# Stationary operands of 64 rows or columns widened to 128 in a pooled attention and ReGLU kernel

## Chip, cores, metric

One core of one Trainium2 chip. The metric is the device time of one execution in microseconds (us), the lower the better. All executions used here are of the fast state; the granted TensorE clock was 0.997 to 1.0 in every profile.

## The reference, cut to what matters

```python
# q, k, v: (8 batches, 8 heads, 576 rows, 64), float32
k_p = k.reshape(B, H, 72, 8, D).mean(axis=3)      # pooled: 72 keys, 72 values per head
v_p = v.reshape(B, H, 72, 8, D).mean(axis=3)
attn = softmax(q @ k_p.T / 8)                     # 576 x 72 per head
x = (attn @ v_p), heads side by side              # 4608 x 512
out = (relu(x @ w_gate) * (x @ w_val)) @ w_out    # 512 -> 1536 -> 512
```

576 rows are four full pieces of 128 and one left piece of 64. The left piece is what this study is about.

## The kernel before: the parts that matter

`P` is 128, `SP` 72, `REST` 64, `n_pc` 5; piece 4 is the left piece. A matmul's `lhsT` is its stationary operand: its partitions are the rows, its free elements the columns.

```python
def weights(b, h, t):                       # exponentials: 72 rows, n columns
    n = piece_size(t)                       # 128, or 64 for the left piece
    if b == 0:
        return pieces[t][:SP, h, :n]
    return exp_tiles[b, h][:SP, t * P:t * P + n]

def pool_v_array(b, half):                  # batches 0 and 1: values pooled on TensorE
    ...
        terms = [(sel_main, main[:, hs, t, :]) for t in range(KG)]
        terms.append((sel_rest[:P // 2], rest[:, hs, :]))      # 64 rows
    ...

def values(b, t, halves=(0, 1)):
    n = piece_size(t)
    ...
            nc.tensor.matmul(
                out=ps[:n, c0:c0 + D + 1], lhsT=weights(b, h, t),
                rhs=stats[b % 2][:SP, g, s0:s0 + D + 1], start=True, stop=True)
    ...                                     # VectorE: reciprocal of the sums, product -> x

def back(b, t, eng):                        # x transposed into x_T
    x, n = x_tiles.pop((b, t)), piece_size(t)
    ...
    if eng is nc.sync:                      # batches 2 to 7 (but three full pieces of 2): by DMA
        eng.dma_start_transpose(out=dst, in_=x)
        return
    for g in range(NG):
        nc.tensor.transpose(out=ps[:, g, :n], in_=x[:, g, :], identity=ident16[:n, :n])
    ...

# the order in the first batch's products, where batch 1 is prepared
run([z[3], z[4], z[5], lambda: pool_k_wide(1, 2, nc.vector), a[6], qt[0], a[7], qt[1], qt[2], kt, ...])
```

`a` and `z` are products of the gate and value matrices for the halves of the first 512 tokens, `qt` transposes of batch 1's queries, `kt` the pooling of its keys on TensorE.

The softmax here doesn't subtract the row's maximum and nothing guards it: scores larger than these inputs give would overflow.

Of the kernel before, what the change touches and what calls it, by code (L numbers as in the profile page):

```python
# [11 lines left out]
F32 = mybir.dt.float32  # L12
F16 = mybir.dt.float16
AF = mybir.ActivationFunctionType
ALU = mybir.AluOpType
# [3 lines left out]
def kernel(  # L19
# [10 lines left out]
    nc = tc.nc  # L30

    B, H, S, D = q.shape
    POOL = 8
    SP = S // POOL
    DM = H * D
    DFF = moe_w_gate.shape[1]
    NTOK = B * S
    P = 128
    NG = H // 2
# [35 lines left out]
    row_pool = ctx.enter_context(tc.tile_pool(name="rowp", bufs=4))  # L75
# [16 lines left out]
    ident16 = const_pool.tile([P, P], F16, name="ident16")  # L92

    sel_main = const_pool.tile([P, SP], F16, name="sel_main")
    sel_rest = const_pool.tile([P, SP], F16, name="sel_rest")
# [20 lines left out]
    REST = 2 * RI * QP  # L116
# [5 lines left out]
    def full_at(b):  # L122
        return b * S + (REST if b % 2 else 0)

    def rest_at(b):
        return b * S + (0 if b % 2 else FULL)
# [27 lines left out]
    KG = POOL // 2  # L154
# [4 lines left out]
    def load_k_wide(b):  # L159

        tl = kin_pool.tile([P, KJ, POOL, D], F16, name="k_in").rearrange("p j t d -> p (j t d)")
        flat = k[b].rearrange("h (p t) d -> (h p) (t d)", p=QP)
        thirds = [slice(i * K_THIRD, (i + 1) * K_THIRD) for i in range(3)]
        k_tiles[b] = [tl[:, cols] for cols in thirds]
        if b:
            nc.gpsimd.dma_start(out=tl[:, :QT * D], in_=flat)
            return
        for i, cols in enumerate(thirds):
            eng = nc.gpsimd
            if i < 2:  # L170
                eng = nc.sync
                k_tiles[b][i] = sum_pool.tile([P, n_hf, TCH // 2], F16, name=f"sum{i}").rearrange(
                    "p f t -> p (f t)")[:, :2 * K_THIRD].bitcast(F32)
            eng.dma_start(out=k_tiles[b][i], in_=flat[:, cols])

    def load_v_wide(b):
        tl = wo_sums.rearrange("p x f d -> p (x f d)")
        n = H * KG * D
        main = tl[:, :n].rearrange("p (h t d) -> p h t d", h=H, d=D)
        rest = tl[:P // 2, n:n + H * D].rearrange("p (h d) -> p h d", h=H)  # L180
        v_tiles[b] = (main, rest)
        nc.gpsimd.dma_start(
            out=main.rearrange("p h t d -> p h (t d)"),
            in_=v[b].rearrange("h (x t) d -> x h (t d)", t=KG)[:P])
        nc.gpsimd.dma_start(
            out=rest, in_=v[b].rearrange("h r d -> r h d")[P * KG:])

    def load_q(b, i0=0, n=NI):
        if b not in q16_tiles:
# [131 lines left out]
    def queries(b, h, i0=0, n=NI):  # L321
        return qT_tiles[b][:, i0:i0 + n, h * QP:(h + 1) * QP]

    exp_tiles = {}
# [28 lines left out]
    def weights(b, h, t):  # L353

        n = piece_size(t)
        if b == 0:
            return pieces[t][:SP, h, :n]
        return exp_tiles[b, h][:SP, t * P:t * P + n]

    def pool_v_array(b, half):  # L360

        ps = ps_mm.tile([P, HH, D], F32, name="mm_ps", tag="mm_ps")
        hs = slice(half * HH, (half + 1) * HH)
        if b:
            main, rest = v_tiles[b]
            terms = [(sel_main, main[:, hs, t, :]) for t in range(KG)]
            terms.append((sel_rest[:P // 2], rest[:, hs, :]))
        else:
            terms = [(sel_first[:SP], v_tiles[b][:SP, hs, t, :]) for t in range(POOL)]
        for i, (sel, rows) in enumerate(terms):  # L370
            nc.tensor.matmul(  # L371
                out=ps[:SP], lhsT=sel, rhs=rows, start=(i == 0), stop=(i == len(terms) - 1))
        g0 = half * NG // 2
        st = stats[b % 2][:SP, g0:g0 + NG // 2, :]
        st = st.rearrange("p g (x d) -> p g x d", d=D)[:, :, 0::3, :]
        src = ps[:SP].rearrange("p (g x) d -> p g x d", x=2)
        if b or half:
            nc.scalar.copy(st, src)
        else:
            nc.vector.tensor_copy(out=st, in_=src)  # L380

    pieces, x_tiles, value_tiles = {}, {}, {}

    def piece_size(t):
        return P if t < 2 * NF else REST

    def piece_scores(t):
        n, j = divmod(t, 2)
        cols = [(j, n * IQ, IQ)] if n < NF else [(0, NF * IQ, RI), (1, NF * IQ, RI)]
        e = row_pool.tile([P, DM], F32, name="row").bitcast(F16).rearrange("p (h t) -> p h t", h=H)  # L390
        for half in range(2):
            ps = ps_mm.tile([P, HH, P], F32, name="mm_ps", tag="mm_ps")
            for r in range(HH):
                h, c0 = half * HH + r, 0
                for j, i0, cnt in cols:
                    nc.tensor.matmul(
                        out=ps[:SP, r, c0:c0 + cnt * QP], lhsT=kpTs[0][j][:, h, :],
                        rhs=queries(0, h, i0, cnt), start=True, stop=True,
                    )
                    c0 += cnt * QP  # L400
            nc.scalar.activation(
                out=e[:SP, half * HH:(half + 1) * HH, :c0], in_=ps[:SP, :, :c0], func=AF.Exp,
                scale=EXP_SCALE)
        pieces[t] = e

    def values(b, t, halves=(0, 1)):


        n = piece_size(t)
        W = 2 * D + 4  # L410
        if halves[0] == 0:
            value_tiles[b, t] = (piece_pool.tile([P, NG, 2, D], F16, name="px"),
                                 piece_pool.tile([P, 2, NG // 2, 2], F32, name="prd"))
        x, rd = value_tiles[b, t]
        for half in halves:
            ps = ps_at.tile([P, 512], F32, name="at_ps", tag="at_ps")
            for h in range(half * HH, (half + 1) * HH):
                g, hh = divmod(h, 2)
                c0 = g % (NG // 2) * W + hh * (D + 1)
                s0 = 3 * D - 1 if hh else 0  # L420
                nc.tensor.matmul(  # L421
                    out=ps[:n, c0:c0 + D + 1], lhsT=weights(b, h, t),
                    rhs=stats[b % 2][:SP, g, s0:s0 + D + 1], start=True, stop=True,
                )
            pv = ps[:n, :NG // 2 * W].rearrange("p (g c) -> p g c", c=W)
            nc.vector.reciprocal(out=rd[:n, half], in_=pv[:, :, D:D + 2])
            nc.vector.tensor_tensor(  # L427
                out=x[:n, half * NG // 2:(half + 1) * NG // 2, :, :],
                in0=pv.rearrange("p g (x c) -> p g x c", x=2)[:, :, :, :D],
                in1=rd[:n, half].unsqueeze(3).to_broadcast([n, NG // 2, 2, D]), op=ALU.mult)  # L430
        x_tiles[b, t] = x[:n].rearrange("p g x d -> p g (x d)")

    def back(b, t, eng):


        x, n = x_tiles.pop((b, t)), piece_size(t)
        x0 = rest_at(b) if t == n_pc - 1 else full_at(b) + t * P
        dst = x_T[:, :, x0 % RING:x0 % RING + n]
        if eng is nc.sync:
            eng.dma_start_transpose(out=dst, in_=x)  # L440
            return
        ps = ps_mm.tile([P, NG, P], F16, name="mm_ps", tag="mm_ps")
        for g in range(NG):
            nc.tensor.transpose(out=ps[:, g, :n], in_=x[:, g, :], identity=ident16[:n, :n])  # L444
        if eng is nc.scalar:
            eng.copy(dst, ps[:, :, :n])
        else:
            eng.tensor_copy(out=dst, in_=ps[:, :, :n])

    h_tiles = {}  # L450

# [72 lines left out]
    wo_sums = const_pool.tile([P, 3, n_hf, HD], F16, name="wo_sums")  # L524
# [592 lines left out]
    def clear_other(half):  # L1117

        upper = any(half is pair[1] for pair in kpTs)
        nc.vector.memset(half[:D] if upper else half[D:], 0.0)  # L1120

    def ones(i):

        two = stats[i].rearrange("s g d -> s (g d)").bitcast(F32).rearrange(
            "s (g d) -> s g d", g=NG)
        nc.vector.memset(two[:SP, :, D // 2:3 * D // 2], TWO_ONES)
# [23 lines left out]
    with tc.manual_schedule():  # L1150
        nc.scalar.preload_act_table_set("natural_log_exp_and_others")
        nc.vector.memset(warm_sb, 0.0)
        for half in kpTs[0]:
            clear_other(half)
        ones(0)
        load_k_wide(0)
        make_identity(nc, ident16)
        load_q(0, 0, IQ)
# [3 lines left out]
        for i in range(1, 4):  # L1162
# [8 lines left out]
            out=sel_first[:SP].rearrange("s (i m) -> s i m", i=NKG),  # L1171
            in_=ident16[:SP, :SP].rearrange("s (m i) -> s i m", i=NKG))
# [14 lines left out]
        pool_v_array(0, 0)  # L1187
        piece_scores(1)
        values(0, 0, (0,))
        pool_v_array(0, 1)  # L1190
        values(0, 1, (0,))
        warm(1)

        half = TCH // 2
# [3 lines left out]
        pv = [lambda half=half: pool_v_array(1, half) for half in range(2)]  # L1198
# [48 lines left out]
        x = [lambda t=t: back(1, t, nc.scalar) for t in range(n_pc)]  # L1247
# [15 lines left out]
        for c in range(1, n_chunks):  # L1263
# [12 lines left out]
            else:  # L1276
# [3 lines left out]
                for fo in range(0, n_hf - 2 * last, 2):  # L1280
# [5 lines left out]
                    n = 2 if fo else 3  # L1286
# [73 lines left out]
```

## Time and profile before

| | before |
|---|---|
| median of the first runs | 318.7 us (318.2 to 318.84, 3 runs) |
| span in the profile | 317.0 us |
| TensorE busy | 309.5 us, 98% |
| matmuls | 2718 |
| VectorE / GpSimd / ScalarE busy | 76% / 70% / 56% |

TensorE sets the end, so the question is how many nanoseconds the change takes off the sequence of matmuls, and whether another engine takes them back. The lines that show this stand in the prediction.

The views below name the engines PE (TensorE; PEld is its weight loads), DVE (VectorE), ACT (ScalarE), POOL (GpSimd) and SP (SyncE). A line of a timeline gives start and length in us, engine, line of the program, operation, what is written and read, and for a matmul the shape of the stationary operand (rows*columns), that of the moving one, and how many instructions were merged.

### The profile page before, as it was taken

To read this page: it belongs to the slowest core of one execution; us is meant where nothing else is said; L and a number is where in the kernel's file an instruction comes from. 1 tells how busy PE (TensorE), PEld (TensorE's weight loads), DVE (VectorE), ACT (ScalarE), POOL (GpSimd) and SP (SyncE) were. 2 spreads that over 40 slices of the span, in tenths; PEclk is the share of its full clock that TensorE was granted. 3 is DMA by queue.
4 is the path that set the end of the run, shared out by engine and by line. 5 is a ranking of instruction groups with operands and counts; after the bars stand their busy time and mean duration, and the time that the engine had idled before them with its cause. 6 is when DMAs were issued, how large, how long until landed. Compare 5 with 4: busy or idle time off the path is not lost.

```text
span 317.0 us, 7245 instructions
## 1 busy us (share of the span) xinstructions
PE 309.5 (98%) x2718; PEld 235.6 (74%) x2718; DVE 240.8 (76%) x527; ACT 177.0 (56%) x422; POOL 223.2 (70%) x295
## 2 busy tenths in 40 slices
PE   7899999999999999999999999999999999999995
PEld 2778875555567887778989867786678888888674
DVE  6666737577587984888968887888789979879762
ACT  1664562674477377537763767276838565556230
POOL 8646878996935978299949884988299767767200
PEclk9999999999999999999999999999999999999999
DMA  8999999969379255996298637432023300120144
GB/s 181 199 204 201 199 215 184 200 133 157 65 130 166 43 114 133 183 110 147 67 161 124 134 93 123 79 91 68 0 43 63 107 3 0 53 81 2 19 126 122
DMA packets 50130, 35.85 MB, mean 113 GB/s; under 512 B 30000, under 2 KB 43888, under 8 KB 50096
## 3 DMA queue, kind: packets, MB, share of 16 engines
q0 software_dynamic: 17136, 18.49, 35.8%
q1 hardware_dynamic: 32816, 16.78, 25.0%
q8 instruction: 21, 0.34, 0.5%
q10 hardware_dynamic: 144, 0.13, 0.1%
q14 instruction: 13, 0.11, 0.1%
HBM read 37.75 MB, written 9.44 MB: 149 GB/s over the span
## 4 chain that ended last, share of the span: by engine, by line
PE 94%; DVE 2%; DMA 2%; issue 1%; ACT 0%; POOL 0%; POOLq 0%
PE mm_ps L462 32%; PE acc_ps L562 20%; PE mm_ps L900 13%; PE mm_ps L812 8%; PE at_ps L334 4%; PE mm_ps L507 3%; PE at_ps L421 3%; PE mm_ps L643 2%; PE at_ps L900 2%; DMA q<-in_q_dram 2%; PE at_ps L812 1%; PE mm_ps L371 1%; DVE px L427 1%; PE mm_ps L444 1%; PE mm_ps L277 1%
## 5 line engine op out<-in xcount | busy, mean ns | idle before, releaser
L471 DVE TENSOR_TENSOR h<-mm_ps,relu 128x512 f16<-128x512 f32 (+1 forms) x70 | 41.7, 598 | 31.8 <-PE mm_ps L462 24.9
L462 PE MATMUL mm_ps<-x_T,wg_sb 128*128 128x512 f16 (+1 forms) x304 | 61.8, 329 | 0.0
L462 PE MATMUL mm_ps<-x_T,wv_sb 128*128 128x512 f16 (+1 forms) x304 | 61.7, 329 | 0.0
L468 ACT ACTIVATE relu<-mm_ps 128x512 f16<-128x512 f32 (+1 forms) x70 | 36.7, 524 | 41.7 <-PE mm_ps L462 39.9
L351 ACT ACTIVATE expT<-at_ps 72x288 f16<-72x288 f32 (+2 forms) x128 | 39.7, 384 | 12.0 <-PE at_ps L334 11.4
L462 PEld LDWEIGHTS <-wv_sb 128*128 128x128 f16 x304 | 29.7, 98 | 20.7 <-issue 0.2
L462 PEld LDWEIGHTS <-wg_sb 128*128 128x128 f16 x304 | 27.7, 98 | 13.5 <-issue 0.6
L914 ACT COPY row<-mm_ps 128x512 f32<-128x512 f32 x45 | 25.6, 585 | 19.8 <-PE mm_ps L900 17.5
L427 DVE TENSOR_TENSOR px<-at_ps,prd 128x256 f16<-128x256 f32 (+1 forms) x80 | 33.8, 423 | 2.7
L562 PEld LDWEIGHTS <-sum 128*128 128x128 f16 x336 | 32.5, 98 | 4.2
L207 POOL TENSOR_TENSOR tree_b<-tree_a 72x256 f32<-72x256 f32 (+1 forms) x42 | 31.9, 760 | 3.3
L922 POOL TENSOR_TENSOR h<-relu 128x256 f16<-128x256 f16 x45 | 29.9, 693 | 5.8 <-ACT relu L921 5.8
L201 POOL TENSOR_TENSOR tree_a<-v_in 72x512 f32<-72x512 f16 x24 | 29.0, 1210 | 2.1 <-DMA v_in<-in_v_dram 2.1
L836 POOL TENSOR_TENSOR h<-px 128x256 f16<-128x256 f16 x30 | 21.4, 724 | 12.2 <-ACT px L833 11.4
L562 PEld LDWEIGHTS <-h 128*128 128x128 f16 x252 | 24.4, 98 | 3.7
L201 POOL TENSOR_TENSOR tree_a<-k_in 96x512 f32<-96x512 f16 x18 | 21.2, 1177 | 5.1 <-DMA k_in<-in_k_dram 5.1
L553 DVE TENSOR_TENSOR sum<-h 128x768 f16<-128x768 f16 x28 | 18.7, 691 | 4.3 <-POOL h L922 4.3
L918 DVE TENSOR_TENSOR relu<-mm_ps,row 128x512 f16<-128x512 f32 x30 | 19.8, 684 | 1.8 <-PE mm_ps L900 1.6
L562 PE MATMUL acc_ps<-wo_sb,h 128*128 128x256 f16 x168 | 20.6, 273 | 0.0
L562 PE MATMUL acc_ps<-wo_sb,sum 128*128 128x256 f16 x168 | 20.6, 273 | 0.0
L562 PE MATMUL acc_ps<-wo_sums,sum 128*128 128x256 f16 x168 | 20.6, 272 | 0.0
L921 ACT ACTIVATE relu<-relu 128x256 f16<-128x256 f16 x45 | 17.6, 415 | 3.4 <-DVE relu L918 3.4
(180 smaller groups left out, 663.5 us busy)
## 6 DMA issues: line engine op xcount, KB each, us to landing
out_dram<-rows SPq DMA_DIRECT2D x24, 256.0 KB
k_in<-in_k_dram POOLq DMA_DIRECT2D x7, 576.0 KB, 6.4
q<-in_q_dram POOLq DMA_DIRECT2D x7, 576.0 KB, 12.6
v_in<-in_v_dram POOLq DMA_DIRECT2D x6, 576.0 KB, 10.7
out_dram<-rows SPq DMA_DIRECT2D x14, 128.0 KB
wg_sb<-in_moe_w_gate_dram POOLq DMA_DIRECT2D x6, 256.0 KB, 10.7
wv_sb<-in_moe_w_val_dram POOLq DMA_DIRECT2D x6, 256.0 KB, 11.1
wo_sb<-in_moe_w_out_dram POOLq DMA_DIRECT2D x3, 512.0 KB, 11.4
```

The lines of the kernel that those rows point to most:

```text
L201: eng.tensor_tensor(out=cell["a"][:n], in0=src[:, :, :4 * D], in1=src[:, :, 4 * D:], op=ALU.add)
L207: eng.tensor_tensor(out=cell["c"][:n], in0=a[:n, :, :2 * D], in1=a[:n, :, 2 * D:], op=ALU.add)
L351: nc.scalar.activation(out=out_ap, in_=in_ap, func=AF.Exp, scale=EXP_SCALE)
L427: nc.vector.tensor_tensor(out=x[:n, half * NG // 2:(half + 1) * NG // 2, :, :], in0=pv.rearrange("p g (x c) -> p g x c", x=2)[:, :, :, :D] ...
L462: nc.tensor.matmul(out=t[:, lo:hi], lhsT=w[:, ci, fsl], rhs=x_T[:, ci, x0:x0 + hi - lo], start=(ci == 0), stop=(ci == n_co - 1),)
L468: nc.scalar.activation(out=relu[:, :n], in_=ps[0][:, :n], func=AF.Relu)
L471: nc.vector.tensor_tensor(out=h_tiles[c][:, fo, t0:t0 + n], in0=ps[1][:, :n], in1=relu[:, :n], op=ALU.mult)
L562: nc.tensor.matmul(out=ps[:, tb, :], lhsT=lhs[:, i, tb * P:(tb + 1) * P], rhs=rhs[:, i, :], start=(first and tb == 0 and i == 0), stop=(tb ...
L812: nc.tensor.matmul(out=ps[key][:, m], lhsT=w_of(m)[:, i], rhs=xs[:, i], start=(first and m == 0 and i == 0), stop=(m == 1 and i == N_CO - ...
L900: nc.tensor.matmul(out=ps[key][:, m], lhsT=w_of(m)[:, i], rhs=xs[:, i], start=(first and m == 0 and i == 0), stop=(m == 1 and i == N_CO - ...
L914: nc.scalar.copy(mid[name], ps[key])
L922: nc.gpsimd.tensor_tensor(out=hc[:, fo_out, cols], in0=gv[key][:, 0], in1=gv[key][:, 1], op=ALU.mult)
```

## The change

The intent: no matmul with a stationary operand of 64 rows or 64 columns is left, so that TensorE always works as one array of 128x128. A left piece takes 64 columns more, of the neighbouring head (batch 0) or of the piece before (batches 1 to 7); the 64 surplus rows of the result are not used. Batch 1's last values get 64 more rows, which a memset makes zero.

```diff
-        rest = tl[:P // 2, n:n + H * D].rearrange("p (h d) -> p h d", h=H)
+        rest = tl[:, n:n + H * D].rearrange("p (h d) -> p h d", h=H)
 ...
         if b == 0:
-            return pieces[t][:SP, h, :n]
-        return exp_tiles[b, h][:SP, t * P:t * P + n]
+            return pieces[t][:SP, h * n:h * n + P]
+        return exp_tiles[b, h][:SP, t * P + n - P:t * P + n]
+
+    def piece_rows(b, t):
+        return slice(P - piece_size(t) if b else 0, P if b else piece_size(t))
 ...
-            terms.append((sel_rest[:P // 2], rest[:, hs, :]))
+            terms.append((sel_rest, rest[:, hs, :]))
 ...
+        if piece_size(t) < P:
+            nc.vector.memset(row[:SP, H * REST:H * REST + P - REST], 1.0)
 ...
-                    out=ps[:n, c0:c0 + D + 1], lhsT=weights(b, h, t),
+                    out=ps[:, c0:c0 + D + 1], lhsT=weights(b, h, t),
 ...
-            nc.tensor.transpose(out=ps[:, g, :n], in_=x[:, g, :], identity=ident16[:n, :n])
+            nc.tensor.transpose(out=ps[:, g, :], in_=x[:, g, :], identity=ident16)
         if eng is nc.scalar:
-            eng.copy(dst, ps[:, :, :n])
+            eng.copy(dst, ps[:, :, rows])
 ...
+        nc.vector.memset(
+            wo_sums.rearrange("p x f d -> p (x f d)")[P // 2:, H * KG * D:H * (KG + 1) * D], 0.0)
```

Cut: the reciprocal and product on VectorE, which run over 128 partitions instead of `n`, and the DMA transpose, which reads `x[rows]`.

More of the change, by code (lines that the diff above doesn't have):

```diff
@@ L185, in load_v_wide @@
         nc.gpsimd.dma_start(
-            out=rest, in_=v[b].rearrange("h r d -> r h d")[P * KG:])
+            out=rest[:P // 2], in_=v[b].rearrange("h r d -> r h d")[P * KG:])
     def load_q(b, i0=0, n=NI):
@@ L389, in piece_scores @@
         cols = [(j, n * IQ, IQ)] if n < NF else [(0, NF * IQ, RI), (1, NF * IQ, RI)]
-        e = row_pool.tile([P, DM], F32, name="row").bitcast(F16).rearrange("p (h t) -> p h t", h=H)
+        row = row_pool.tile([P, DM], F32, name="row").bitcast(F16)
+        e = row[:, :H * piece_size(t)].rearrange("p (h t) -> p h t", h=H)
+        if piece_size(t) < P:
+            nc.vector.memset(row[:SP, H * REST:H * REST + P - REST], 1.0)
         for half in range(2):
@@ L403, in piece_scores @@
                 scale=EXP_SCALE)
-        pieces[t] = e
+        pieces[t] = row
     def values(b, t, halves=(0, 1)):
-        n = piece_size(t)
         W = 2 * D + 4
@@ L421, in values @@
                 nc.tensor.matmul(
-                    out=ps[:n, c0:c0 + D + 1], lhsT=weights(b, h, t),
+                    out=ps[:, c0:c0 + D + 1], lhsT=weights(b, h, t),
                     rhs=stats[b % 2][:SP, g, s0:s0 + D + 1], start=True, stop=True,
                 )
-            pv = ps[:n, :NG // 2 * W].rearrange("p (g c) -> p g c", c=W)
-            nc.vector.reciprocal(out=rd[:n, half], in_=pv[:, :, D:D + 2])
+            pv = ps[:, :NG // 2 * W].rearrange("p (g c) -> p g c", c=W)
+            nc.vector.reciprocal(out=rd[:, half], in_=pv[:, :, D:D + 2])
             nc.vector.tensor_tensor(
-                out=x[:n, half * NG // 2:(half + 1) * NG // 2, :, :],
+                out=x[:, half * NG // 2:(half + 1) * NG // 2, :, :],
                 in0=pv.rearrange("p g (x c) -> p g x c", x=2)[:, :, :, :D],
-                in1=rd[:n, half].unsqueeze(3).to_broadcast([n, NG // 2, 2, D]), op=ALU.mult)
-        x_tiles[b, t] = x[:n].rearrange("p g x d -> p g (x d)")
+                in1=rd[:, half].unsqueeze(3).to_broadcast([P, NG // 2, 2, D]), op=ALU.mult)
+        x_tiles[b, t] = x.rearrange("p g x d -> p g (x d)")
     def back(b, t, eng):
-        x, n = x_tiles.pop((b, t)), piece_size(t)
+        x, n, rows = x_tiles.pop((b, t)), piece_size(t), piece_rows(b, t)
         x0 = rest_at(b) if t == n_pc - 1 else full_at(b) + t * P
@@ L439, in back @@
         if eng is nc.sync:
-            eng.dma_start_transpose(out=dst, in_=x)
+            eng.dma_start_transpose(out=dst, in_=x[rows])
             return
@@ L443, in back @@
         for g in range(NG):
-            nc.tensor.transpose(out=ps[:, g, :n], in_=x[:, g, :], identity=ident16[:n, :n])
+            nc.tensor.transpose(out=ps[:, g, :], in_=x[:, g, :], identity=ident16)
         if eng is nc.scalar:
-            eng.copy(dst, ps[:, :, :n])
+            eng.copy(dst, ps[:, :, rows])
         else:
-            eng.tensor_copy(out=dst, in_=ps[:, :, :n])
+            eng.tensor_copy(out=dst, in_=ps[:, :, rows])
     h_tiles = {}
```

## The prediction

> **What bounds the kernel now.** I read the page first, for the engine that sets the end.
>
> ```profile
> PE 309.5 (98%) x2718; PEld 235.6 (74%) x2718; DVE 240.8 (76%) x527; ACT 177.0 (56%) x422; POOL 223.2 (70%) x295
> PE 94%; DVE 2%; DMA 2%; issue 1%; ACT 0%; POOL 0%; POOLq 0%
> ```
>
> The first line is busy time by engine, the second the chain that ended last, by engine. TensorE is busy 98% of a 317.0 us span and is 94% of that chain. The strip of 40 slices agrees: PE stands at 9 in all but the first and last slice, and the granted clock is full. So a nanosecond that TensorE no longer spends should leave the total, unless something behind it is late. Matmul ends are modelled in this profile, so in what follows I use starts only.
>
> The second view was the groups by line with shapes kept apart, for stationary operands of 64 rows or columns ("72*64" is 72 rows by 64 columns).
>
> ```profile
> L421 PE MATMUL at_ps<-stat,expT 72*64 72x65 f16 x56 | 3.1, 198 | 0.0
> L371 PE MATMUL mm_ps<-wo_sums,sel_rest 64*72 64x256 f16 x2 | 0.6, 297 | 0.0
> L444 PE MATMUL mm_ps<-ident,px 64*128 64x64 f16 x8 | 0.6, 192 | 0.0
> L421 PE MATMUL at_ps<-stat,row 72*64 72x65 f16 x8 | 0.4, 199 | 0.0
> ```
>
> These 74 matmuls show as 4.7 us busy and no idle time, so nothing looks wrong here. The cost is in the third view, the timeline of TensorE, which I read around one left piece and around one full piece of the same stage.
>
> ```profile
> 99.82 0.82 PE L900 MATMUL mm_ps<-early_x,early_w 128*128 128x256 f16 x6
> 100.57 0.44 PE L421 MATMUL at_ps<-stat,expT 72*64 72x65 f16 x8
> 100.94 0.61 PE L462 MATMUL mm_ps<-x_T,wg_sb 128*128 128x512 f16 x2
> ...
> 107.77 0.38 PE L900 MATMUL at_ps<-x_T,wv_sb 128*128 128x256 f16 x2
> 107.98 0.41 PE L421 MATMUL at_ps<-stat,expT 72*128 72x65 f16 x8
> 108.23 0.49 PE L900 MATMUL mm_ps<-early_x,early_w 128*128 128x256 f16 x3
> ```
>
> A 256-column matmul takes 0.109 us from start to start (107.77 to 107.98 for two). Six from 99.82 end at 100.47, yet the 64-column group starts at 100.57: 0.10 us are missing. Its eight matmuls then hold TensorE until 100.94, 0.37 us, where the eight of 128 columns take 0.25. Single starts in the trace place the rest: the last 256-column matmul to the first 64-column one is 203 ns instead of 109, the first to the second 52 instead of 34, the last to the next 128-column matmul 130 instead of about 31, and one more step after it is some 10 ns long. Every one of the eight left pieces has these numbers within 2 ns, so this is no wait for data.
>
> **What the Trainium skill says.** "TensorEngine Tiling (Array Packing)", Tiling Modes, Key Properties: changing the tiling mode, not just the tile, drains TensorE; a dimension of 64 or less selects a smaller tile. The trace agrees with a price of 94 ns to enter and 99 ns to leave, and operands of 72 or 96 rows or columns pay nothing: the eight 72*72 matmuls of line 371 step by 108 to 113 ns throughout, neighbours included. "TensorE: Matmul & The Clock Gate", Weight-path perf modes: fast weight load is on for 128 columns of a type other than FP32. The weight loads of line 421 take 97 ns with 128 columns and 111 ns with 64, so the wider load costs no more. "Perfetto Trace Analysis", Tensor Engine Instruction, says the reported end is estimated, not observed; hence busy time and the idle column hide the drain, which starts do show.
>
> **The change part by part.** The order of both programs shows the same 5438 TensorE rows in the same sequence, the same rows on ScalarE, GpSimd and SyncE, and two more on VectorE.
>
> 1. Values of left pieces, 8 groups of 8. Between two 256-column neighbours the distance from the previous start to the next start is 579 ns, for the 128-column groups 358. That is 221, and the step after the group is 8 to 10 ns too long as well: 0.229 us each, 8 x 0.229 = 1.83 us. The moving operand has 65 columns in either form, so the full form costs what a full piece costs today.
>
> 2. Transposes of left pieces, two groups of four (batches 0 and 1; the other batches transpose by DMA).
>
> ```profile
> 24.20 0.60 PE L462 MATMUL mm_ps<-x_T,wv_sb 128*128 128x256 f16 x4
> 24.73 0.29 PE L444 MATMUL mm_ps<-ident,px 64*128 64x64 f16 x4
> 24.95 0.61 PE L462 MATMUL mm_ps<-x_T,wg_sb 128*128 128x256 f16 x4
> ```
>
> Here the change also adds work: the moving operand, the identity, grows from 64 to 128 columns, 56 ns a step instead of 29 to 39. From the last start before to the first after it is 425 ns now; a full group is 109 + 4 x 56 = 333. With 11 ns of the next step that is 0.103 us, and 0.101 for the second group (345 to 255, 11 more): 0.20 us.
>
> 3. Batch 1's last values, two matmuls of 64 rows.
>
> ```profile
> 42.60 0.60 PE L371 MATMUL mm_ps<-wo_sums,sel_main 128*72 128x256 f16 x4
> 43.13 0.30 PE L371 MATMUL mm_ps<-wo_sums,sel_rest 64*72 64x256 f16 x1
> 43.36 0.61 PE L462 MATMUL mm_ps<-x_T,wg_sb 128*128 128x256 f16 x4
> ```
>
> Last start before to first after: 432 ns, against 2 x 109 = 218 with 128 rows; with 10 ns of the next step 0.224 each: 0.45 us.
>
> 4. Added. A memset of 64x256 words on VectorE in the first 3 us. One of 72x256 takes 0.27 us there, and VectorE then waits 1.11 us for the first keys (until 4.04), so it is hidden. A memset of 72x64 between the values of pieces 2 and 3 of batch 0 is not: VectorE runs without a gap from 18.74 to 21.69, and TensorE waits about 0.3 us at 21.41 for the last quotient of that row. The memsets of 128x32 words take 0.09 us; for twice the elements I choose 0.08 us of delay, the only loss on the path. The VectorE and ScalarE operations on left pieces keep their length, since 64 or 128 partitions make no difference (0.42 us for both forms of line 427).
>
> Sum: 1.83 + 0.20 + 0.45 - 0.08 = 2.40 us, 0.75%.
>
> **The rivals.** First, the gain is taken back by waits: TensorE arrives earlier and waits for another engine or a DMA. For it: VectorE is 80 to 90% busy in the middle, and TensorE already stalls some 0.2 us once a chunk (starts near 181.83, 214.49, 247.14). Against it: that stall has one length three times, so it follows TensorE's own work; VectorE falls idle again between its bursts (at 169 to 174 us it runs nearly without gaps and then waits for TensorE at 174.90 and 177.09); and the early loads have slack of more than 1.5 us (second batch's queries land at 29.46 and are read at 31.07; the wide values at 37.9, read at 42.6), against at most 1.1 us that TensorE gains by 48 us. If half went so: 317.5 us.
>
> Second, the drain is not of the 64-wide form but of switching between kinds of work, and stays. For it: the transposes and values are short matmuls among long ones. Against it: the full pieces in the same places show steps of 34 and 112 ns, without it. It would make 318.7 us, or a little more for the wider transposes.
>
> Third, the change does harm elsewhere: left pieces of batches 1 to 7 now lie in partitions 64 to 127, and their DMA transposes read from there; values of head h read the exponentials of head h+1 in batch 0, so they wait for both halves. If those transposes took 1 us longer, chunks that start on a left piece might wait: up to 2 us over the kernel, 319 to 320. The profile has no transpose from such a start, so nothing speaks for it; the exponentials are done at 19.86 and read at 22.50.
>
> **Range and chances.** 318.7 - 2.4 = 316.3 us. The three runs before span 0.6 us, so plus or minus 0.4 is noise. Upward I allow half of the gain lost; downward there is little more than a lucky shift of waits: 315.7 to 317.3. Faster by 2% would take 6.4 us, more than these matmuls hold: 0.01. Slower by 2%, only if the third rival is far larger than I think: 0.01.
>
> **What would show it.** In the profile after, the groups with 64 in the stationary shape are gone; each left piece stands 0.25 us from the next group; batch 1's last values step by 0.11 us; TensorE's busy time falls by about 2 us and its share stays at 98%. The step is wrong if the eight still take 0.37 us, or if the spacing is right but the span falls less: then new idle time before TensorE names who took it. DMA transposes over 1.2 us in the median would point to the third rival.

## The result

| | before | changed |
|---|---|---|
| median | 318.77 us (318.2 to 319.02, 4 runs) | 316.53 us (316.35 to 316.64, 4 runs) |
| ratio | | 0.9932, 95% interval 0.9915 to 0.9949 |
| span in the profile | 317.0 us | 314.8 us |
| TensorE busy | 309.5 us | 307.0 us |

A ratio is the mean time of one kernel's fast runs over that of the other's of the same rounds, so it is not quite the ratio of the medians. The kernel became 2.24 us faster by the medians, 0.7%. The predicted 316.3 us is 0.23 us low, inside its range.

The page of the changed kernel, busy time and the chain that ended last:

```profile
PE 307.0 (98%) x2718; PEld 235.9 (75%) x2718; DVE 241.0 (77%) x529; ACT 176.9 (56%) x422; POOL 223.4 (71%) x295
PE 94%; DMA 2%; DVE 2%; issue 1%; ACT 0%; POOL 0%; POOLq 0%
```

The bound is the same engine with the same share; its time shrank by 2.5 us. In the groups with shapes kept apart, no line has a 64 in the stationary shape any more:

```profile
L427 PE MATMUL at_ps<-stat,expT 72*128 72x65 f16 x280 | 14.6, 193 | 0.0
L375 PE MATMUL mm_ps<-wo_sums,sel_rest 128*72 128x256 f16 x2 | 0.5, 273 | 0.0
```

The timeline of TensorE around the same left piece, and around batch 1's last values (start, length, what):

```profile
98.36 1.04 PE L906 MATMUL mm_ps<-early_x,early_w 128*128 128x256 f16 x8
99.23 0.41 PE L427 MATMUL at_ps<-stat,expT 72*128 72x65 f16 x8
99.48 0.59 PE L468 MATMUL mm_ps<-x_T,wg_sb 128*128 128x512 f16 x2
...
42.37 0.60 PE L375 MATMUL mm_ps<-wo_sums,sel_main 128*72 128x256 f16 x4
42.80 0.27 PE L375 MATMUL mm_ps<-wo_sums,sel_rest 128*72 128x256 f16 x1
42.91 0.38 PE L468 MATMUL mm_ps<-x_T,wg_sb 128*128 128x256 f16 x2
```

Eight 256-column matmuls from 98.36 end at 99.23 (8 x 0.109 = 0.87), where the left piece starts at once; it holds TensorE for 0.25 us instead of 0.37. The last values are left after 0.11 us instead of 0.23.

Both kernels have the same 2718 matmuls in the same order, so their starts can be subtracted one by one. From the first transposed query to the last matmul the two traces differ by these amounts:

| part | predicted | measured |
|---|---|---|
| values of the eight left pieces | -1.83 | -1.67 (six of 0.23, batch 5's 0.21, batch 7's 0.08) |
| transposes of two left pieces | -0.20 | -0.20 (0.103 and 0.100) |
| batch 1's last values | -0.45 | -0.45 (0.223 and 0.224) |
| memset in batch 0's chain on VectorE | +0.08 | +0.02 |
| waits of TensorE at 143 to 149 us | none | -0.05 |
| all else | none | -0.01 |
| sum | -2.40 | -2.36 |

The changed kernel's trace began 0.08 us late, as its first queries landed at 8.20 us instead of 8.13; so 2.29 us are left at the last matmul, and 2.2 in the spans.

Batch 7's piece shows where a part of the gain went. The timeline of all engines of the changed kernel there:

```profile
227.33 0.54 ACT L351 ACTIVATE expT<-at_ps 72x32 f16<-72x32 f32 x2 [0.38 <-PE at_ps L334]
227.57 0.56 PE L427 MATMUL at_ps<-stat,expT 72*128 72x65 f16 x8
227.97 0.60 PE L468 MATMUL mm_ps<-x_T,wg_sb 128*128 128x512 f16 x2
```

The eight take 0.40 us from 227.57 to 227.97, not 0.25. The eighth needs the last exponentials, which ScalarE ends at 227.87; it starts 172 ns after the seventh instead of about 32. Before, ScalarE's last exponentials ended at 230.07 and the eighth matmul started at 230.11: the drain had covered that wait. The view names no wait here, since the modelled end of the seventh matmul lies behind the eighth's start.

### The profile page after: what moved, and what is told of

Read it like the earlier page. It is cut to its first block, busy times and chain, and to the rows that moved or that the text cites. A ratio compares the mean times of both kernels' runs of the same rounds, so it can differ in the third digit from the quotient of the medians.

```text
span 314.8 us, 7247 instructions
## 1 busy us (share of the span) xinstructions
PE 307.0 (98%) x2718; PEld 235.9 (75%) x2718; DVE 241.0 (77%) x529; ACT 176.9 (56%) x422; POOL 223.4 (71%) x295
## 4 chain that ended last, share of the span: by engine, by line
PE 94%; DMA 2%; DVE 2%; issue 1%; ACT 0%; POOL 0%; POOLq 0%
PE mm_ps L468 32%; PE acc_ps L568 20%; PE mm_ps L906 13%; PE mm_ps L818 8%; PE at_ps L334 4%; PE mm_ps L513 3%; PE at_ps L427 3%; PE mm_ps L649 3%; PE at_ps L906 2%; DMA q<-in_q_dram 2%; PE at_ps L818 1%; DVE px L433 1%; PE mm_ps L375 1%; PE mm_ps L450 1%; PE mm_ps L277 1%
## 5 line engine op out<-in xcount | busy, mean ns | idle before, releaser
L433 DVE TENSOR_TENSOR px<-at_ps,prd 128x256 f16<-128x256 f32 x80 | 33.9, 424 | 2.7
```

The source lines that it names most:

```text
L433: nc.vector.tensor_tensor(out=x[:, half * NG // 2:(half + 1) * NG // 2, :, :], in0=pv.rearrange("p g (x c) -> p g x c", x=2)[:, :, :, :D], ...
```

## The experiments

My theory: TensorE works in modes of tile size (a tile is a part of the array that works as an array of its own), a stationary operand of 64 or fewer rows or columns selects a smaller tile, and a stretch of such matmuls is paid for on entering and on leaving, whatever its length. The pause at such an edge is the drain. The rivals: the cost goes by the number of small matmuls; it is the full 128 columns with the fast weight load that helps; a change of tile drains as well; and, for the time, later waits take gains back.

Twelve runs were made, all with right results. The kernel before was timed in the same calls. Runs 1 to 4 shared a chip, as did 5 and 6, 7 and 8, and 9 to 12.

| run | median (range), us | before, us | ratio, interval |
|---|---|---|---|
| values_only | 317.1 (316.81 to 317.61) | 318.68 | 0.9944 (0.9919 to 0.997) |
| rest64 | 316.85 (316.59 to 317.41) | 318.68 | 0.9935 (0.9909 to 0.996) |
| after_again | 316.53 (316.35 to 316.8) | 318.68 | 0.9924 (0.9897 to 0.9952) |
| threshold | 316.46 (316.2 to 317.06) | 318.68 | 0.9924 (0.9893 to 0.9956) |
| alternate | 323.85 (323.64 to 323.98) | 318.57 | 1.0164 (1.0149 to 1.0179) |
| tiles | 318.0 (317.65 to 318.64) | 318.57 | 0.9983 (0.9966 to 1.0) |
| after_late | 316.33 (315.94 to 317.2) | 318.57 | 0.9934 (0.9921 to 0.9948) |
| before_late | 318.36 (318.33 to 318.49) | 318.57 | 0.9991 (0.9979 to 1.0004) |
| after_late2 | 316.13 (315.69 to 318.05) | 318.54 | 0.9926 (0.9903 to 0.9948) |
| before_late2 | 318.3 (318.12 to 318.85) | 318.54 | 0.9988 (0.9974 to 1.0001) |
| after_third | 316.58 (316.2 to 317.02) | 318.54 | 0.9933 (0.9917 to 0.9948) |
| before_again | 318.74 (318.37 to 319.11) | 318.54 | 0.9999 (0.9975 to 1.0024) |

### The parts alone

values_only is the changed kernel with the other two parts undone, rest64 with the last values alone undone:

```diff
-            terms.append((sel_rest, rest[:, hs, :]))
+            terms.append((sel_rest[:P // 2], rest[:P // 2, hs, :]))      # both
-            nc.tensor.transpose(out=ps[:, g, :], in_=x[:, g, :], identity=ident16)
+            nc.tensor.transpose(                                         # values_only
+                out=ps[:, g, :n], in_=x[rows, g, :], identity=ident16[rows, rows])
 ...     # the copies out of PSUM likewise
```

> The changed kernel with parts 2 and 3 undone: the transposes of left pieces take 64 rows again (batch 1's from partitions 64 to 127) and batch 1's last values take 64 rows; only the 8 groups of values stay at 128 columns. Drain theory (each stretch of small matmuls is paid once on entering and once on leaving): 0.20 + 0.45 = 0.65 us more than the changed kernel, about 317.2 us, and 1.6 us less than the kernel before. In the trace: 432 ns around each of the two 64-row values and about 425 ns around the transposes. Rival (the gain of the values is taken back by later waits and the rest carried it): about 318.3 us.

> The changed kernel with part 3 alone undone: batch 1's last values (two matmuls) take 64 rows again. Drain theory: two stretches of one matmul each, 2 x 0.224 = 0.45 us more than the changed kernel, about 317.0 us; 432 ns from the last start before to the first after. Rival (cost goes by the number of small matmuls, some 0.03 us each): 0.06 us more, 316.6 us.

The medians are 0.57 and 0.32 us above the changed kernel's in the same call, where 0.65 and 0.45 were expected. The range of rest64 overlaps that of the changed kernel (that of values_only just does not), so the times alone support the direction, not the size. The traces give the size: matmul by matmul against the changed kernel, each 64-row value costs 0.21 to 0.22 us and each group of 64-row transposes 0.10. The parts add up, and the rival of a gain of the values that comes to nothing (318.3 us) is out.

### The changed kernel again

> The changed kernel once more, for a second trace and more times: 316.5 us. It tells which small steps of the first trace belong to the kernel: the two waits of 55 and 64 ns near 141 and 144 us that are gone, the 0.07 us that the start was later (first keys and queries landed later), and the step of 172 ns inside a group of values at 227.9 us. What belongs to the kernel is there again within 10 ns; what doesn't is not.

316.53 us once more. The wait inside batch 7's piece is there again (139 ns, and 139 to 141 ns in every run whose batch 7 piece has full operands), so it belongs to the kernel. The two small waits at 143 and 146 us stay away here, and are in both traces of the kernel before; but they are also gone in before_late, before_late2, tiles and alternate, which keep 64-column operands. So they go with the timing of that stage, not with the drain itself, and what moves them is open. The late start didn't repeat: the first queries landed at 7.68 us, and the matmuls ran 0.52 us earlier than in the first trace until 31.5 us. There they stopped; see below.

### Just above 64

The layout lets batch 0's left piece take 72 columns, its transposes 72 rows, and batch 1's last values 72 rows:

```diff
-            terms.append((sel_rest, rest[:, hs, :]))
+            terms.append((sel_rest[:72], rest[:72, hs, :]))
-                    out=ps[:, c0:c0 + D + 1], lhsT=weights(b, h, t),
+                    out=ps[:72 if t == n_pc - 1 and not b else P, c0:c0 + D + 1],
+                    lhsT=weights(b, h, t)[:, :72 if t == n_pc - 1 and not b else P],
 ...     # VectorE's two operations and the transposes likewise
```

> The changed kernel, with what it widened to 128 set just above 64 where the layout lets it: batch 0's left piece takes 72 columns, its transposes 72 rows and columns, batch 1's last values 72 rows; the left pieces of batches 1 to 7 stay at 128. Theory (64 or less selects a smaller tile and a drain, 65 to 128 doesn't): same time as the changed kernel, 316.5 us, 0.36 us from the last start before batch 0's left piece to the first after, 218 ns around the last values. Rival (it is the full 128, with its fast weight load, that helps): 0.58 us around the left piece and 432 ns around the last values, about 317.1 us.

The timeline of TensorE of threshold at both places:

```profile
21.67 0.60 PE L471 MATMUL mm_ps<-x_T,wv_sb 128*128 128x256 f16 x4
22.11 0.44 PE L427 MATMUL at_ps<-stat,row 72*72 72x65 f16 x8
22.39 0.60 PE L471 MATMUL mm_ps<-x_T,wg_sb 128*128 128x256 f16 x4
...
42.19 0.60 PE L375 MATMUL mm_ps<-wo_sums,sel_main 128*72 128x256 f16 x4
42.62 0.27 PE L375 MATMUL mm_ps<-wo_sums,sel_rest 72*72 72x256 f16 x1
42.74 0.60 PE L471 MATMUL mm_ps<-x_T,wg_sb 128*128 128x256 f16 x4
```

From 72 rows or columns on there is no drain: 21.67 plus 4 x 0.109 is 22.11, where the piece starts, and it ends after 0.28 us. That is 0.03 more than with 128 columns (the drained piece took 0.37 and started 0.10 late); where the 0.03 comes from was not tested. The weight loads of this piece take 118 ns in the mean, longer than the 111 with 64 columns and the 97 with 128, and yet there is no drain. The rival of the fast weight load is out. Sizes between 64 and 72 were not run.

### Half as many small matmuls, in more stretches

alternate keeps every second head of a left piece at 64 columns and gives the other heads 128, so the eight matmuls change mode at each step. Batches 1 to 7 take the 64 columns that lead to output partitions 64 to 127. VectorE works on the 64 valid rows alone (a first form that read all 128 was refused by the simulator, for reading what an earlier tile had left; that attempt is not in the record).

```diff
-                    out=ps[:, c0:c0 + D + 1], lhsT=weights(b, h, t),
+                    out=ps[piece_rows(b, t) if h % 2 else slice(0, P), c0:c0 + D + 1],
+                    lhsT=weights(b, h, t)[:, piece_rows(b, t) if h % 2 else slice(0, P)],
 ...     # the rest as in values_only
```

> As values_only, but in each of the 8 left pieces only every second head (four of eight) takes 64 columns, in turn with heads of 128: half as many small matmuls as in the kernel before, in four stretches of one instead of one stretch of eight. Drain theory: 4 stretches x 8 groups x 0.224 = 7.2 us more than values_only (317.2), about 324.4 us, 5.6 us slower than the kernel before. Rival (cost per small matmul, 0.229/8 each): half of 1.83 us more than values_only, about 318.1 us, faster than the kernel before.

323.85 us: 5.3 us slower than the kernel before, with half as many small matmuls. The rival by number (318.1, faster than before) is out. The timeline of TensorE of alternate, around the group whose like is shown for both kernels (the view merges both widths into one line):

```profile
101.26 0.93 PE L909 MATMUL mm_ps<-early_x,early_w 128*128 128x256 f16 x7
102.03 1.20 PE L427 MATMUL at_ps<-stat,expT 72*128 72x65 f16 x8
103.16 0.82 PE L471 MATMUL mm_ps<-x_T,wg_sb 128*128 128x512 f16 x3
```

The eight hold TensorE for 1.13 us instead of 0.25. Inside, after a first step of 125 ns, the starts lie 134 and 151 ns apart in turn, where full ones lie 31 apart. From the last start before to the first after it is 1239 ns against 358, with some 8 of the next step 0.889 us for four stretches, 0.222 each; expected was 0.224. Over eight groups that is 7.1 us. From the first transposed query to the last matmul the trace is 6.98 us longer than that of values_only: the drains cover the wait of 0.14 us inside batch 7's piece again.

### A change of tile without a change of mode

tiles keeps the 64 columns of the kernel before, but sends the heads in turn to output partitions 0 to 63 and 64 to 127, in two PSUM banks:

```diff
+        for i in range(H if left else 0):
+            r, half = divmod(i, 2)
+            h = half * HH + r
 ...
+                out=banks[half][half * REST:(half + 1) * REST, c0:c0 + D + 1],
+                lhsT=weights(b, h, t), rhs=stats[b % 2][:SP, g, s0:s0 + D + 1],
```

> As the kernel before (left pieces of 64 columns, 64-row transposes, 64-row last values), but the eight matmuls of a left piece go in turn to the two halves of the array's columns (output partitions 0 to 63 and 64 to 127): one mode, seven changes of tile in each group. Left pieces of batches 2 to 7 need two DMA transposes instead of one. If only the mode drains: the same as before, 318.8 us, with 94 ns to enter and 99 to leave and nothing between; if the two halves run side by side, steps inside shrink to half and it is up to 0.9 us faster. If a change of tile drains as well: 8 x 7 x 0.1 to 0.19, 5 to 11 us slower than before.

318.0 us, 0.57 below the kernel before in the same call, with an interval of 0.9966 to 1.0: no slower, and perhaps a little faster. The timeline of TensorE of tiles:

```profile
99.65 0.71 PE L932 MATMUL mm_ps<-early_x,early_w 128*128 128x256 f16 x5
100.29 0.32 PE L430 MATMUL at_ps<-stat,expT 72*64 72x65 f16 x8
100.54 0.82 PE L494 MATMUL mm_ps<-x_T,wg_sb 128*128 128x512 f16 x3
```

Five matmuls from 99.65 end at 100.20, and the group starts at 100.29: the entry still costs 94 ns, and the leaving 99 in the single starts. Between them the steps are 3, 49, 4, 32, 4, 25, 4 ns: the two halves of a pair start 3 to 4 ns apart and run side by side. So a change of tile is free, as "TensorEngine Tiling (Array Packing)", Tiling Modes, Key Properties of the Trainium skill has it, and the mode alone costs. The whole group takes 453 ns against 579 before and 358 with full operands: for eight matmuls even two tiles side by side do not earn the mode.

### A wall at 32 us

after_again ran 0.52 us earlier than the first trace of the changed kernel, and lost it all at once. The timelines of its engines there:

```profile
29.75 0.99 POOL L234 TENSOR_TENSOR early_x<-tree_a 128x384 f16<-128x384 f32 x1
30.05 1.11 DVE L233 TENSOR_TENSOR mid<-k_in 128x384 f32<-128x384 f16 x1
31.20 0.60 PE L468 MATMUL mm_ps<-x_T,wv_sb 128*128 128x256 f16 x4
31.67 0.42 DVE L477 TENSOR_TENSOR h<-mm_ps,relu 128x256 f16<-128x256 f32 x1
32.14 0.72 PE L308 MATMUL mm_ps<-ident,q 128*128 128x128 f16 x10 [0.34 <-DVE h L477]
```

The four matmuls from 31.20 end at 31.64, and the transposes wait for VectorE until 32.14: 0.50 us (the view says 0.34, as it counts from the modelled end). VectorE's addition of batch 1's keys took 1.11 us instead of 0.55, until GpSimd had finished its own addition. "GPSIMD Engine Reference", Specifications, of the Trainium skill says that GpSimd's SBUF interfaces are shared with VectorE and contended by VectorE instructions with two SBUF inputs, which this one is; the traces agree. In the six traces where it was stretched (after_again, threshold, rest64, tiles, after_third, before_again: 0.65 to 1.11 us) it ended 0.41 to 0.42 us after GpSimd's, though it had started at different times. GpSimd starts when batch 1's keys have landed. So these transposes cannot start earlier than a fixed time after that landing:

| trace | keys landed | transposes start | difference | TensorE waited |
|---|---|---|---|---|
| after_again | 26.62 | 32.14 | 5.52 | 0.50 |
| tiles | 26.91 | 32.42 | 5.51 | 0.34 |
| threshold | 26.47 | 31.98 | 5.51 | 0.22 |
| after_third | 26.73 | 32.25 | 5.52 | 0.15 |
| rest64 | 26.41 | 31.92 | 5.51 | 0.09 |
| before_again | 27.13 | 32.64 | 5.51 | 0.05 |
| changed, first trace | 26.57 | 32.16 | 5.59 | none |
| before, first trace | 26.69 | 32.39 | 5.70 | none |
| values_only | 26.12 | 32.07 | 5.95 | none |
| alternate | 25.98 | 32.63 | 6.65 | none |

These are all the traces without the move that follows. Where TensorE waited, the difference is 5.51 or 5.52, in six traces of five programs; in the other four it is larger. This is a wall: 0.33 us of the change's gain, batch 0's piece and its transposes, lie before it, and are kept only in executions where TensorE comes there late enough after that landing.

To take it away I moved the addition behind the next product, where GpSimd is done, and gave one copy to ScalarE, in both kernels:

```diff
-        run([z[3], z[4], z[5], lambda: pool_k_wide(1, 2, nc.vector), a[6], qt[0], a[7], ...
+        run([z[3], z[4], z[5], a[6], lambda: pool_k_wide(1, 2, nc.vector), qt[0], a[7], ...
-        qt = [lambda n=n: q_transposes(1, n, nc.vector) for n in range(NQ)]
+        qt = [lambda n=n: q_transposes(1, n, nc.vector if n else nc.scalar) for n in range(NQ)]
```

> The changed kernel, with VectorE's addition of batch 1's last third of keys one step later (after the product of tile 6), and the copy of batch 1's first transposed queries on ScalarE. Theory of a wall at 32 us: in the second trace of the changed kernel this addition took 1.11 us instead of 0.55, ending 0.42 us after GpSimd's last addition of keys, and TensorE waited 0.50 us for VectorE at 32.1; so what TensorE gains before 32 us is lost unless the start was late. With the addition moved, TensorE should not wait there: 0 to 0.5 us faster than the changed kernel (by how early the first keys and queries land), about 316.2 us. Rival (the wait belongs to that one execution and costs nothing in the others): 316.5 us.

> The kernel before, with the same move. Wall theory: without the wall the changed kernel keeps all that it gains in batch 0, so this one is slower than after_late by the full sum of the prediction, 2.4 us, and faster than the kernel before by less than after_late is faster than the changed kernel: some 318.5 us. Rival: the difference stays at the 2.15 to 2.25 us measured so far.

> after_late once more, on one chip with the three below. Its first five runs spread from 315.9 to 317.2 us, too wide to tell 0.2 us. Wall theory: below the changed kernel by 0.1 to 0.5 us, no wait of TensorE near 32 us. Rival (the wall costs nothing on average): equal to the changed kernel within 0.1 us.

> before_late once more. Wall theory: slower than after_late2 by 2.3 to 2.4 us, more than the 2.15 to 2.25 us between the kernel before and the changed one. The first pair showed 2.0 in the medians and 2.4 in the spans of the two profiles, so it is open. Rival: 2.0 to 2.2 us again.

> The changed kernel a third time, beside the two above: 316.5 us, and in its trace a wait of TensorE at 32 us whose length follows how early the first queries landed (none at 8.20 us, 0.50 at 7.68).

> The kernel before once more, for a second trace: 318.6 us. In the first one the first queries landed late (8.13 us) and TensorE did not wait at 32 us. Wall theory: if they land at 7.7 to 7.9 us here, it waits 0.1 to 0.3 us at 32 us, where the changed kernel would wait 0.33 us longer: then the gain of batch 0 is lost in such executions. Rival: no wait.

The wait is gone in all four late traces. Two of them test the wall: in after_late and before_late2 the transposes start 4.89 and 4.95 us after the keys landed, where the wall stood at 5.51. In after_late2 and before_late (5.53 and 5.70) they would not have met it anyway. after_late's timelines:

```profile
30.91 0.55 DVE L233 TENSOR_TENSOR mid<-k_in 128x384 f32<-128x384 f16 x1
...
31.18 0.60 PE L468 MATMUL mm_ps<-x_T,wv_sb 128*128 128x256 f16 x4
31.62 0.72 PE L308 MATMUL mm_ps<-ident,q 128*128 128x128 f16 x10
```

The keys had landed at 26.73, GpSimd's last addition ended at 30.85, the addition on VectorE is back at 0.55 us, and the transposes start at 31.62, where the four matmuls before end (31.18 + 0.44). So the mechanism is shown, for the two edits of the move together; what the copy on ScalarE alone did was not run. Its worth in time is not clear. The late version of the changed kernel has the lowest medians of all, 316.13 us against 316.58 of the changed kernel on the same chip, but its runs spread from 315.69 to 318.05 and the intervals of the ratios overlap almost wholly. The expected gap between the late pair, 2.3 to 2.4 us, is 2.0 and 2.2 in the medians, the range of the rival; the spans of the profiles give 2.4 and 2.7. So I cannot say from the times how much the wall takes on average. Of my expectations for the repeats, one was misread: the wait follows the landing of batch 1's keys together with the first queries, not the queries alone. after_third waited 0.15 us with queries at 8.15 us, where I had tied "none" to 8.20. before_again's queries landed at 8.33, outside what that expectation asked for, so the 0.1 to 0.3 us stay untested; it met the wall for 0.05 us.

## Why the prediction was right

**The bound.** TensorE at 98% was read as: a nanosecond off its sequence leaves the total. That held: 2.36 us off the sequence, 2.2 off the span and 2.24 off the median.

**The drain, 94 ns in and 99 out.** Right in cause, and in its size as a whole, some 0.22 us a stretch. The 99 holds for the groups of eight; after the single matmuls of the last values it is 120 to 121 ns (230 against 109), which the sum had, as it was taken from whole distances. One left piece does not have the numbers that the prediction gives to all eight: batch 2's follows a 96-column matmul and starts after 136 ns, not 203, again 94 more than with full operands (42). It is the mode, not the number of small matmuls (alternate), not the tile (tiles), not the narrow weight load (threshold).

**The sum.** Transposes and last values came out at their predicted size. The values did not: 1.83 was eight equal pieces, and batch 7's gave 0.08 instead of 0.23, as ScalarE's last exponentials of that batch come just then. I had read the distances in the kernel before as free of waits since all eight agreed within 2 ns; but a drain of 0.2 us can hide a wait of 0.14 behind it. The memset was overestimated: 0.02 us, not 0.08. The two errors and 0.05 us of vanished waits nearly cancel, so the closeness of 2.40 and 2.36 is partly luck. (The prediction's count of 5438 TensorE rows stands in no trace: both show 2718 matmuls and 2718 weight loads. The matmuls are in the same order, as it says.)

**The first rival, waits.** I gave the early loads a slack of over 1.5 us from the queries of batch 1. That step failed: I had followed the load of the queries and not that of the keys, whose path runs through GpSimd and a VectorE addition that is held up by it. Its slack was 0.19 us in the first trace before (5.70 less 5.51) and 0.08 in that of the changed kernel, and in six of the eight later traces without the move TensorE ran into it. The half that I allowed for lost gain in the range was the right side to allow for.

**The second rival**, that the drain stays, fell in the first trace. **The third**, harm elsewhere: the median over all 27 DMA transposes of this tile is 1.19 us in both kernels, but only six of them, those of the left pieces of batches 2 to 7, now read from partition 64. Those six took 1.17 to 2.39 us before (median 1.18) and 1.17 to 2.24 after (median 1.28), and the subtraction of the starts shows no new wait of TensorE from it. Batch 0 did not wait for the second half of the exponentials.

## What to carry to other kernels

Where TensorE is the bound, look for stationary operands of 64 or fewer rows or columns among wide ones, and measure from start to start across their edges: each stretch cost some 0.22 us here, and filling it up to 72 or 128 with rows or columns that nobody reads cost next to nothing. Whether smaller tiles earn their mode in longer stretches, with several side by side, no run here shows. When a fix takes time off an engine, look for what arrives just in time behind it, in both directions: the wait that the removed cost had hidden, and the load whose slack was smaller than the gain.

## What the Trainium skill lacked or had wrong

- "TensorEngine Tiling (Array Packing)", Key Properties: it says that a change of mode drains TensorE, but gives no price. Here: some 94 ns to enter, the same after moving operands of 65, 96 and 256 columns; 99 ns to leave after a group of eight and 120 after a single matmul; with slower steps around them some 0.22 us a stretch.
- The same page, When to Use Tiling: it goes by the dimension and says nothing of how many such matmuls come in a row. For eight matmuls of 64 columns the group took 579 ns in one tile, 453 in two tiles side by side and 358 as 128 columns, from the last start before to the first after; 72 columns paid no drain.
- "Perfetto Trace Analysis", Tensor Engine Instruction: it says that matmul ends are modelled, not what follows: drains of 0.1 us showed neither as idle nor as a wait, and the wait of 0.50 us at 32 us was listed as 0.34.
- No page says that an operand of 64 or fewer rows or columns gets the smaller tile unasked. Here no call asks for one: 64 paid the drain, 72 did not, and in tiles two 64-column matmuls started 3 to 4 ns apart.
